# Attention in front of two dense layers on one core: half-height TensorE tiles for units 3 to 11, a new written order, and 40 dummy matmuls

## The chip, the cores and the metric

The kernel runs on one core of one Trainium2 chip, in one launch. The metric is the device time of that core in microseconds (us). A core has five engines that each work through their own queue in order: TensorE (PE, matmuls; its weight loads are listed as PEld), VectorE (DVE), ScalarE (ACT), GpSimd (POOL) and SyncE (SP, which issues most DMAs).

## The reference

```
# 4 batches, 8 heads, 576 positions, head size 64; q and k are drawn 8 times larger
scores = (q @ k.T) / 8
mask:  heads 0-3: 0 <= i-j < 32;  heads 4-7: 0 <= i-j < 128 and (i-j) % 4 == 0
x = softmax(where(mask, scores, -1e9)) @ v          # -> 2304 tokens x 512
h = x @ moe_w_in                                    # 512 -> 2048
x = (h - tanh(h)) @ moe_w_out                       # 2048 -> 512
a, b = x @ moe2_w1, x @ moe2_w2                     # 512 -> 1024 each
out = ((a * b) @ moe2_w3) @ moe2_w_out              # 1024 -> 1024 -> 512
```

q, k and v are float32; the weights come as 64-bit words and are turned into float32 on the chip.

## The kernel before, in words

**Units.** Attention is cut into 12 units: 4 batches times 3 blocks of 192 query positions (3 tiles of 64). Each unit does all 8 heads, as two types: `p` (plain heads 0 to 3) and `d` (dilated heads 4 to 7). A type has two pairs of heads (`e`), a pair has two heads (`h`). A query tile of 64 is handled as two halves of 32 (`half`), and each half looks at a window of 64 keys.

**Steps of a unit**, each a letter in the written order. `q` and `v` load keys with queries, and values (SP). `s` computes scores (lines 480 to 512): one bfloat16 matmul with an identity writes the mask into a PSUM bank, then 24 float32 matmuls for a type add the scores, each in a column tile of 32 (`tile_position=(0, 32*j)`, four of them). The queries lie zero-padded over 128 rows (64 of one head, 64 of the other), so a matmul uses all 128 rows although half of its weights are zeros. A float32 matmul is two instructions in the trace, so a type is 48 and a unit 96. `M` takes the row maximum and subtracts it (DVE), `E` is the exponential (ACT), `N` sums and inverts (DVE), `m` multiplies (POOL), `T` transposes on TensorE (3 per type), `C` copies the transposed weights out of PSUM (lines 568 to 577), twice per type: each copy multiplies by a 0/1 column of `sel_sb`, so that the rows of the other pair are zero. `P` multiplies by the values (lines 579 to 596): 12 float32 matmuls per type with 128 rows, 64 columns and 64 moving elements (24 instructions). `X` and `L` split the result into a rounded part and a rest in the big tile `X` (ACT, DVE).

Units 0 to 2 (`n < PB`) run one type at a time; from unit 3 on `s`, `M`, `E`, `N` and `m` take both types in one step, and the two score banks belong to one tile `both`.

**The first dense layer** is cut into 4 groups of the hidden size. Group 0 has 3 chunks and 8 token tiles, 24 steps: `h` (12 matmuls), `t` tanh (ACT), `g` difference (DVE), `G` rounded part (ACT), `k` rest (POOL), `y` (12 matmuls into the output banks), `Y` and `Z` (bank to SBUF). `h0` needs the attention of batch 0, which is units 0 to 2; `h6` needs that of units 3 to 5, and so on. Group 0 runs interleaved with attention, by hand. Weights for groups 0 and 1 are prepared in the same stretch: `w` load, `a` absolute value (ACT), `b` two and `c` two passes over the bits (DVE, lines 149 to 162), `i` rounded part (ACT), `o` rest (POOL).

**What sets the order.** The string `ORDER` (lines 49 to 69) has 504 words; `first_group` (lines 756 to 817) emits them one after the other, and each engine runs its own in that order. There is no scheduler behind it: a word that waits holds up all later work of its engine. `S<n>` (`spin`, line 750) exists but is not used in this order: it takes an `h` bank and writes `n` bfloat16 matmuls of 512 columns into it that nobody reads. After group 0 loops write the steps: groups 1 to 3 (to about 470 us), eight products of the two last weight matrices (to 521 us), then three passes over token pairs.

**The h banks.** `h_tile` (lines 624 to 627) counts its calls in `nh`. Until `Q0` (`close_attn`) all calls get the one bank of pool `hA`. From then on a call whose count is a multiple of 4 gets `hA`, the others one of three banks of `yB["h"]` in turn. The last eight calls are the eight products (line 935); each is read by ACT (line 945) and DVE (line 946). Line 967 then takes the banks for the last stage, the `hA` bank first; the first matmul of the last stage writes into it.

**PSUM in attention.** `bank_of` (lines 468 to 478) places the scores of units 0 to 2: the first two in the two banks of pool `psS`, the next two in the `y` banks, the last two in `psS` again, which waits until both earlier ones are read.

Of the kernel before, what the change touches and what calls it, by code (L numbers as in the profile page):

```python
# [8 lines left out]
F32 = mybir.dt.float32  # L9
# [26 lines left out]
R = 4  # L36
# [14 lines left out]
N2p T1p v0p s1d v1p m2p s2d w1 a0 E0d C1p T2p b0 P0p C2p N0d c0 M1d X0p M2d E1d v2p a1 m0d L0p b1  # L51
T0d q3p E2d P1p C0d w2 a2 q3d P2p N1d c1 m1d T1d s3 N2d C1d i0 m2d i1 T2d b2 c2 v0d v1d X1p L1p w3
P0d o0 X2p L2p o1 X0d i2 M3 P1d L0d X1d E3 a3 L1d q4p q4d h0 v2d s4 N3 C2d P2d w4 b3 t0 g0 h1 G0 c3
i3 X2d M4 t1 a4 m3p T3p k0 o2 L2d q5p E4 q5d g1 o3 y0 w5 h2 v3p q6p G1 s5 C3p v3d b4 c4 t2 k1 m3d
T3d g2 q6d i4 o4 a5 N4 C3d h3 m4p M5 t3 E5 b5 P3p c5 v4p T4p v4d C4p y1 N5 X3p L3p g3 P3d G2 X3d m4d
T4d i5 k2 C4d L3d s6 M6 q7p q7d o5 P4p v5p X4p L4p h4 t4 m5p y2 Y2 G3 E6 P4d X4d w6 g4 h5 T5p Z2 C5p
m5d s7 N6 G4 L4d v5d P5p k3 y3 t5 g5 a6 X5p G5 T5d C5d w7 k4 a7 b6 k5 v6p m6p L5p y4 h6 M7 q8p t6
T6p c6 g6 q8d y5 q9p C6p i6 h7 G6 v6d E7 b7 t7 c7 g7 P5d N7 k6 w8 G7 Y5 m6d s8 q9d X5d P6p X6p Z5
T6d k7 h8 v7p m7p y6 L5d C6d P6d t8 M8 a8 E8 g8 G8 q10p m7d h9 N8 m8p X6d v7d T7p C7p s9 T7d o6 k8
t9 g9 y7 C7d h10 M9 t10 L6p g10 T8p G9 v8p E9 i7 N9 b8 P7p L6d X7p w9 y8 h11 k9 m8d L7p Y8 q10d s10  # L60
q11p G10 t11 C8p m9p P7d g11 q11d Z8 X7d P8p X8p L7d L8p T8d k10 y9 G11 M10 h12 c8 y10 E10 k11 C8d
t12 v8d m9d v9p a9 v9d y11 w10 T9p C9p g12 h13 G12 P8d b9 Y11 k12 Z11 t13 N10 m10p g13 T9d m10d G13
s11 M11 P9p X8d L8d C9d X9p k13 c9 E11 y12 w11 T10p h14 y13 C10p T10d t14 g14 a10 b10 G14 P9d k14
N11 m11p L9p C10d v10p h15 t15 v10d y14 g15 G15 Y14 h16 v11p T11p t16 k15 Z14 g16 y15 X9d o7 L9d G16
k16 m11d P10p X10p h17 C11p c10 t17 v11d P10d g17 G17 y16 L10p X10d T11d C11d h18 a11 t18 P11p X11p
L10d L11p P11d k17 X11d w12 g18 y17 L11d Y17 b11 Q0 i8 G18 i9 c11 h19 Z17 k18 t19 o8 g19 h20 G19 h21
w13 t20 y18 k19 i10 y19 h22 g20 t21 g21 G20 G21 k20 i11 k21 y20 a12 h23 b12 o9 a13 b13 t22 g22 G22
o10 o11 Z20 k22 Y20 h24 c12 t23 c13 g23 i12 y21 G23 y22 o12 k23 i13 y23 t24 g24 G24 o13 k24 Z23 Y23
"""


# [9 lines left out]
def attn_moe_kernel(  # L81
# [358 lines left out]
    def window(t, half):  # L440

        return 32 * half if t else 0

    def load_v(n, parts=AB):
        if n < NU:
            b, g = units[n]
            for ty in parts:
                v = v_home(n).rearrange("p (h t c) -> p h t c", h=2, t=TU)
                for e in range(2):

                    for t0, t1 in ((0, 1), (1, TU)) if g == 0 else ((0, TU),):
                        src = vt[b, 2 * ty + e, :HW, TU * g + t0:TU * g + t1].rearrange("k t c -> k (t c)")
                        ap = [list(d) for d in src.ap]
                        step = ap[0][0] * window(TU * g + t0, 1)
                        nc.sync.dma_start(
                            out=v[e:128:2, :, t0:t1].rearrange("k h t c -> k h (t c)"),
                            in_=bass.AP(tensor=src.tensor, offset=src.offset, ap=[ap[0], [step, 2], ap[1]]),
                        )
                vs[n, ty] = v

    NB = 2 * TU

# [16 lines left out]

    def at_scores(n, parts=AB):  # L480
        b, g = units[n]
        if n not in ust:
            ms = attn_pools["sm"].tile([128, 2, 2, NB], F32, tag="ms", name="ms")
            if n == 2:
                pm = Yf[:, KC * NT - 6 * KW - 2 * NB * HW:KC * NT - 6 * KW]
                pm = pm.rearrange("p (u i k e) -> p u i k e", u=2, i=TU, e=2)
            else:
                pm = attn_pools["pp"].tile([128, 2, TU, HW, 2], F32, tag="pm", name="pm")
# [3 lines left out]
        ps = ust[n]["ps"]  # L492
        for ty in parts:
            ps[ty] = bank_of(n, ty)[:, :NB * HW].rearrange("p (i k e) -> p i k e", i=TU, e=2)
            m0 = (M_DIL if ty else M_PLAIN)[g]
            nc.tensor.matmul(
                out=ps[ty], lhsT=id16_sb,
                rhs=mask_sb[:, m0:m0 + TU].unsqueeze(3).to_broadcast([128, TU, HW, 2]),
                start=True, stop=False, skip_group_check=True,
            )  # L500
# [10 lines left out]
                            skip_group_check=True, tile_position=(0, HQ * j),  # L511
                        )

    def of_parts(n, parts):

        s = ust[n]
        if len(parts) == 2:
            both = s["both"][:, :, :NB * HW].rearrange("p u (i k e) -> p u i k e", i=TU, e=2)
            return [(both, s["mx"], s["pm"], [128, 2, TU, HW, 2])]
        return [(s["ps"][u], s["mx"][:, u], s["pm"][:, u], [128, TU, HW, 2]) for u in parts]  # L520

    def at_max(n, parts=AB):
        for ps, mx, pm, shape in of_parts(n, parts):
            both = len(shape) == 5
            mx = mx.rearrange("p u (i e) -> p u i e" if both else "p (i e) -> p i e", e=2)
            nc.vector.tensor_reduce(
                out=mx, in_=ps.rearrange("p u i k e -> p u i e k" if both else "p i k e -> p i e k"), axis=AX.X, op=ALU.max
            )
            nc.vector.tensor_tensor(
                out=pm, in0=ps, in1=mx.unsqueeze(len(shape) - 2).to_broadcast(shape), op=ALU.subtract  # L530
            )

    def at_exp(n, parts=AB):
# [2 lines left out]

    def at_norm(n, parts=AB):
        s = ust[n]
        pm, sm = (s["pm"], s["sm"]) if len(parts) == 2 else (s["pm"][:, parts[0]], s["sm"][:, parts[0]])
        both = len(parts) == 2  # L540
        nc.vector.tensor_reduce(  # L541
            out=sm.rearrange("p u (i e) -> p (u i) e" if both else "p (i e) -> p i e", e=2),
            in_=pm.rearrange("p u i k e -> p (u i) e k" if both else "p i k e -> p i e k"), axis=AX.X, op=ALU.add
        )
        nc.vector.tensor_scalar(out=sm, in0=sm, scalar1=1e-9, scalar2=None, op0=ALU.add)
        nc.vector.reciprocal(out=sm, in_=sm)

    def at_mult(n, parts=AB):
        s = ust[n]
        for u in parts:  # L550
            nc.gpsimd.tensor_tensor(
                out=s["pm"][:, u], in0=s["pm"][:, u],
                in1=s["sm"][:, u].rearrange("p (i e) -> p i e", e=2).unsqueeze(2).to_broadcast([128, TU, HW, 2]),
                op=ALU.mult,
            )

    def at_T(n, parts=AB):
        for u in parts:
# [9 lines left out]
    def at_Tcopy(n, parts=AB):  # L568
        for u in parts:
            pt = ust[n]["pt"][u]  # L570
            pb = ust[n]["pt"][u] = attn_pools["pb"][:, npb[0] % NPB]
            npb[0] += 1
            for e in range(2):
                nc.scalar.activation(
                    out=pb[:, :, :, e], in_=pt.rearrange("p i (j q) -> p i j q", j=4), func=ACTF.Copy,
                    scale=sel_sb[:, e:e + 1],
                )

    def at_pv(n, parts=AB):
# [598 lines left out]
```

## Time and profile before

| | us |
|---|---|
| median of 3 runs (lowest, highest) | 800.28 (800.1, 801.37) |
| the profiled execution, and its span from first to last instruction | 802.01, 800.2 |
| PE busy (matmul instructions) | 779.9 |
| PEld busy | 688.0 |
| DVE busy | 548.1 |
| ACT busy | 292.8 |
| POOL busy | 158.3 |

Busy means that at least one instruction of the engine is under way; a wait is idle time. [...] The time outside the span (802.01 less 800.2) is start and end of the launch.

### The profile page before, as it was taken

Reading aid. Unit: us, or ns where it says so; the run is one execution under the profiler, and the core shown is the slowest. Engines: PE = TensorE matmul, PEld = TensorE weight load, DVE = VectorE, ACT = ScalarE, POOL = GpSimd, SP = SyncE. Lnnn points to the kernel's source line nnn. Section 1 sums busy time; section 2 is a strip of 40 time slices with the busy share of each in tenths; the row PEclk is TensorE's granted clock in tenths of the full one; section 3 lists DMA queues with packets and bytes.
Section 4 is the critical chain, followed back from the end, with each engine's and each line's share of the span. In section 5 each row is a group of like instructions: output and inputs, shape, how many; then the busy total and the mean of one; then the engine's idle time right before and its main releaser. Section 6 shows DMA issues by size and latency. Waiting matters only on the chain.

```text
span 800.2 us, 14174 instructions
## 1 busy us (share of the span) xinstructions
PE 779.9 (97%) x5592; PEld 688.0 (86%) x5592; DVE 548.1 (68%) x909; ACT 292.8 (37%) x546; POOL 158.3 (20%) x153
## 2 busy tenths in 40 slices
PE   5699999999999999999999999999999999999998
PEld 4589999888889888898888898799998999899996
DVE  4998675668888779987888889954454544734431
ACT  3566565443444444444444444321122111311111
POOL 3363343500022001210022223211121111211111
PEclk9799999999999999999999999999999999999999
DMA  9988742114455253632554344296203750156302
GB/s 300 302 247 294 236 155 73 53 53 126 150 160 158 105 162 116 186 119 66 156 155 136 105 134 131 93 340 211 93 1 115 238 187 1 41 181 202 118 1 79
DMA packets 62018, 115.58 MB, mean 144 GB/s; under 512 B 6400, under 2 KB 27008, under 8 KB 61952
## 3 DMA queue, kind: packets, MB, share of 16 engines
q1 hardware_dynamic: 61664, 114.32, 44.8%
q8 instruction: 44, 0.72, 0.4%
q10 hardware_dynamic: 288, 0.36, 0.2%
q14 instruction: 22, 0.18, 0.1%
HBM read 95.26 MB, written 19.40 MB: 143 GB/s over the span
## 4 chain that ended last, share of the span: by engine, by line
PE 89%; DVE 8%; ACT 1%; DMA 1%; issue 1%; ACTq 0%; SPq 0%; DVEq 0%
PE h L635 26%; PE y L725 25%; PE pr L979 22%; PE o L1042 6%; PE pr L1042 6%; PE x L592 2%; DVE a L159 2%; PE s L508 2%; DVE a L162 1%; DVE a L153 1%; PE t L561 1%; DVE a L149 1%; DVE Y L872 1%; DVE ms L541 1%; DMA id_sb<-in_ident 0%
## 5 line engine op out<-in xcount | busy, mean ns | idle before, releaser
L725 PE MATMUL y<-gs,LT 128*128 128x512 f32 (+1 forms) x520 | 121.9, 368 | 0.0
L725 PEld LDWEIGHTS y<-gs,LT 128*128 128x128 f32 x520 | 92.1, 188 | 16.3
L635 PE MATMUL h<-X,LT 128*128 128x512 f32 (+1 forms) x471 | 104.9, 370 | 0.0
L635 PEld LDWEIGHTS h<-X,LT 128*128 128x128 f32 x471 | 82.8, 188 | 15.2
L683 DVE TENSOR_TENSOR th<-h,th 128x512 f32<-128x512 f32 (+1 forms) x83 | 51.3, 618 | 58.5 <-ACT th L677 58.3
L979 PE MATMUL pr<-X 128*128 128x384 f32 x435 | 81.8, 334 | 0.0
L979 PE MATMUL pr<-X,LT 128*128 128x384 f32 x405 | 80.7, 336 | 0.0
L635 PE MATMUL h<-X,w 128*128 128x512 f32 (+1 forms) x381 | 78.8, 352 | 0.0
L677 ACT ACTIVATE th<-h 128x512 f32<-128x512 f32 (+1 forms) x83 | 44.8, 540 | 87.4 <-PE h L635 87.4
L979 PEld LDWEIGHTS pr<-X 128*128 128x128 f32 x435 | 76.2, 188 | 0.5
L159 DVE SCALAR_TENSOR_TENSOR a<-st,a 128x512 uint32<-128x512 uint32 x68 | 75.2, 1107 | 0.3
L979 PEld LDWEIGHTS pr<-X,LT 128*128 128x128 f32 x405 | 71.9, 188 | 1.3
L635 PEld LDWEIGHTS h<-X,w 128*128 128x128 f32 x381 | 62.8, 188 | 10.6 <-DVE th L683 0.2
L690 ACT ACTIVATE gs<-th 128x512 fp32r<-128x512 f32 (+1 forms) x83 | 47.9, 577 | 64.5 <-DVE th L683 57.5
L1016 DVE TENSOR_TENSOR u<-pr,u 128x384 f32<-128x384 f32 x72 | 40.1, 557 | 45.1 <-PE pr L979 38.5
L725 PE MATMUL y<-gs,w 128*128 128x256 f32 (+1 forms) x352 | 70.4, 330 | 0.0
L144 ACT ACTIVATE a<-st 128x512 f32<-128x512 f32 x68 | 45.5, 670 | 59.7 <-DMA st<-in_w 21.0
L992 ACT ACTIVATE cs<-u 128x384 fp32r<-128x384 f32 x24 | 12.6, 526 | 149.4 <-DVE u L1016 149.4
L1034 POOL TENSOR_TENSOR Y<-w,v 128x384 f32<-128x384 f32 x24 | 24.5, 1019 | 212.8 <-DVE w L1016 212.8
L725 PEld LDWEIGHTS y<-gs,w 128*128 128x128 f32 x352 | 54.6, 188 | 6.5
L162 DVE SCALAR_TENSOR_TENSOR a<-st,a 128x512 uint32<-128x512 uint32 x68 | 54.8, 806 | 2.3
L170 POOL TENSOR_TENSOR LT<-a,LT 128x512 fp32r<-128x512 f32 x18 | 25.8, 1436 | 152.2 <-ACT LT L167 152.2
(169 smaller groups left out, 1259.5 us busy)
## 6 DMA issues: line engine op xcount, KB each, us to landing
st<-in_w SPq DMA_DIRECT2D x28, 512.0 KB, 3.5
LT<-p SPq DMA_DIRECT2D x56, 256.0 KB, 4.2
X<-p SPq DMA_DIRECT2D x56, 256.0 KB, 4.7
st<-in_w_in SPq DMA_DIRECT2D x16, 512.0 KB, 4.2
st<-in_w_out SPq DMA_DIRECT2D x16, 512.0 KB, 4.1
q<-in_qz SPq DMA_DIRECT2D x18, 384.0 KB, 5.3
p<-LT SPq DMA_DIRECT2D x26, 256.0 KB, 4.5
v<-in_vt SPq DMA_DIRECT2D x32, 192.0 KB, 4.6
```

The costliest lines, as they stand in the source:

```text
L144: nc.scalar.activation(out=a.bitcast(F32), in_=st[:, :, 1].bitcast(F32), func=ACTF.Abs)
L159: nc.vector.scalar_tensor_tensor(out=a, in0=st[:, :, 1], scalar=0xC0000000, in1=a, op0=ALU.bitwise_and, op1=ALU.bitwise_or)
L162: nc.vector.scalar_tensor_tensor(out=a, in0=st[:, :, 0], scalar=29, in1=a, op0=ALU.logical_shift_right, op1=ALU.bitwise_or)
L170: nc.gpsimd.tensor_tensor(out=lo, in0=a.bitcast(F32), in1=hi.bitcast(F32), op=ALU.subtract)
L635: nc.tensor.matmul(out=ps, lhsT=a[sel[0]], rhs=b[sel[1]], start=(start and i == 0), stop=(i == n - 1), **kw)
L677: nc.scalar.activation(out=th[:, :tn], in_=gst[i][:, :tn], func=ACTF.Tanh)
L683: nc.vector.tensor_tensor(out=th[:, :tn], in0=ps[:, :tn], in1=th[:, :tn], op=ALU.subtract)
L690: nc.scalar.activation(out=gs[:, 0, :tn], in_=th[:, :tn], func=ACTF.Copy)
L725: nc.tensor.matmul(out=y[k], lhsT=wt[sel[0]][:, 128 * k:128 * k + 128], rhs=gs[:, sel[1], tn * m:tn * m + tn], start=(cs[m] == 0 and n == ...
L979: nc.tensor.matmul(out=ps[:, :TP], lhsT=s[e][:, 128 * k:128 * k + 128], rhs=(hi, lo)[f][1][k], start=start and n == 0, stop=n == 5, skip_g ...
L1016: nc.vector.tensor_tensor(out=out, in0=ps[:, :TP], in1=x, op=op)
L1042: nc.tensor.matmul(out=tiles[m], lhsT=cs[e][:, 128 * m:128 * m + 128], rhs=WW[j][f], start=begin and n == 0, stop=end and n == 2,)
```

## The change

Four things change together.

1. From unit 3 on a score matmul uses the 64 rows of its own head alone: `tile_position=(64*h, 32*j)`, so there are eight tiles of 64 rows and 32 columns; the two heads (the two row halves) write to two different banks. The number of matmuls stays 48 for a unit. Rows of the score tile are now (pair, query), columns (tile, type, key).
2. `C` becomes one copy per head without `sel_sb` (2 instead of 4 for a unit). `P` takes both types in one step: 48 matmuls with 64 rows, 64 columns and 32 moving elements instead of 24 with 128 rows and 64 moving elements, on four tiles of 64 x 64; the two types (the two row halves) write to two banks. The value loads fill 64 neighbouring rows instead of every second row.
3. `bank_of` gives units 0 to 2 the banks psS0, y0, y1, psS1, y0, y1.
4. `ORDER` is rewritten: the same words but for `P` (one for a unit from unit 3 on) and nine `S` words with 14, 3, 3, 2, 4, 4, 3, 4 and 3 dummy matmuls, all ahead of `h0`. The first weights are loaded and their bits prepared ahead of the masks; scores of units 3 and 4 both stand ahead of `h0` (before: unit 3 alone), `b3 c3` and `N3` too.

```diff
-K0 K1 q0p q1p s0p q2p q0d M0p q1d s1p E0p s2p s0d M1p N0p m0p w0 T0p E1p C0p N1p M2p q2d M0d E2p m1p
...
-P0d o0 X2p L2p o1 X0d i2 M3 P1d L0d X1d E3 a3 L1d q4p q4d h0 v2d s4 N3 C2d P2d w4 b3 t0 g0 h1 G0 c3
...
+w0 q0p q1p w1 q2p q0d a0 b0 K0 K1 c0 S14 s0p s1p s2p q1d q2d a1 w2 M0p v0p E0p M1p i0 b1 c1 s0d M2p
+N0p E1p E2p m0p i1 M0d v1p s1d E0d N1p m1p a2 S3 T0p M1d C0p N2p E1d m2p s2d q3p q3d v2p S3 T1p P0p
+C1p S2 T2p C2p N0d M2d X0p w3 m0d b2 P1p N1d q4p m1d s3 o0 o1 X1p c2 L0p L1p T0d C0d v0d a3 S4 T1d
+P2p E2d X2p S4 P0d q4d v1d M3 E3 S3 s4 v2d b3 c3 i2 L2p C1d N2d N3 X0d m2d w4 P1d L0d X1d q5p m3p S4
+T2d C2d L1d a4 S3 h0 M4 t0 g0 P2d q5d T3p b4 E4 o2 w5 i3 N4 G0 m3d h1 s5 C3p o3 t1 k0 T3d g1 v3p v3d
...
     def bank_of(n, ty):
 
-        if n >= PB:
-            return ust[n]["both"][:, ty]
         m = order0.index((n, ty))
-        if 2 <= m < 4:
-
-            return yA.tile([128, 2, 256], F32, tag=f"y{m - 2}", name=f"s{m}").rearrange("p a c -> p (a c)")
-        if m % 4 == 0:
+        if m % 3:
+            y = yA.tile([128, 2, 256], F32, tag=f"y{m % 3 - 1}", name=f"s{m}")
+            return y.rearrange("p a c -> p (a c)")
+        if m == 0:
             banks0["s"] = attn_pools["psS"].tile([128, 2, 512], F32, tag="s", name="s")
-        return banks0["s"][:, m % 2]
+        return banks0["s"][:, m // 3]
...
+    def scores_by_rows(n, g):
+
+        ps = ust[n]["both"][:, :, :NB * HW].rearrange("p h (i u k) -> p h i u k", i=TU, u=2)
...
+        for i in range(TU):
+            t = TU * g + i
+            for ty in AB:
+                k, q = kq[ty]
+                for h in range(2):
+                    r = slice(64 * h, 64 * h + 64)
+                    for e in range(2):
+                        for half in range(2):
+                            k0 = KS[t] - KS[TU * g] + window(t, half)
+                            j, c = 2 * e + half, QT * h + HQ * half
+                            nc.tensor.matmul(
+                                out=ps[HQ * j:HQ * j + HQ, h, i, 1 - ty], lhsT=q[r, e, i, c:c + HQ],
+                                rhs=k[r, e, k0:k0 + HW], start=False, stop=(i == TU - 1 and ty == 1),
+                                skip_group_check=True, tile_position=(64 * h, HQ * j),
+                            )
...
     def at_Tcopy(n, parts=AB):
...
+            if n >= PB:
+                pb = ust[n]["pt"][u] = pb.rearrange("p i j e q -> p (i j e q)")[:, :TU * 128]
+                nc.scalar.activation(out=pb, in_=pt.rearrange("p i c -> p (i c)"), func=ACTF.Copy)
+                continue
...
     def at_pv(n, parts=AB):
...
+        for i in range(TU):
+            for half in range(2):
+                for e in range(2 if n >= PB else 0):
+                    for ty in AB:
+                        r = slice(HW * (1 - ty), HW * (1 - ty) + HW)
+                        for h in range(2):
+                            c = 128 * i + QT * e + HQ * half
+                            nc.tensor.matmul(
+                                out=x_part(n, ty, i, half, h)[:, e], lhsT=v[e][r, half, i, D * h:D * h + D],
+                                rhs=s["pt"][h][r, c:c + HQ], start=True, stop=True,
+                                tile_position=(r.start, 64 * h),
+                            )
```

## Rows read from the trace of the kernel before

**Rows 1.** The page: busy tenths of PE, DVE and granted clock in 40 slices.
```profile
PE   5699999999999999999999999999999999999998
DVE  4998675668888779987888889954454544734431
PEclk9799999999999999999999999999999999999999
```

**Rows 2.** Busy time by stretch: us, then each engine's busy time (instructions), PEclk, DMA.
```profile
0.00:36.85 36.85, 21.29 (x530) 16.60 (x530) 26.26 (x52) 15.11 (x30) 12.23 (x24) 0.89 0.93 297
36.85:60.00 23.15, 22.74 (x488) 20.29 (x487) 21.56 (x37) 15.27 (x31) 13.18 (x13) 0.95 0.83 260
60.00:157.45 97.45, 97.45 (x1400) 89.76 (x1399) 65.11 (x114) 57.08 (x125) 40.60 (x41) 1.00 0.52 167
...
30.00:40.00 10.00, 7.45 (x97) 6.24 (x92) 8.96 (x14) 5.09 (x11) 3.21 (x3) 0.54 0.97 322
```

**Rows 3.** Timeline of PE, 34 to 44 us: start, us, line, out<-in, count, idle before.
```profile
34.10 2.83 PE L592 MATMUL x<-pb,v 128*64 128x64 f32 x48 [2.55 <-DVE X L619]
36.85 2.83 PE L635 MATMUL h<-X,WG 128*128 128x256 f32 x12
39.53 0.50 PE L496 MATMUL s<-mask_sb,id_sb 128*128 128x384 bf16 x2
39.96 1.55 PE L508 MATMUL s<-k,q 128*32 128x64 f32 x96
41.44 0.92 PE L592 MATMUL x<-pb,v 128*64 128x64 f32 x24
42.28 1.69 PE L635 MATMUL h<-X,WG 128*128 128x256 f32 x12
43.81 0.49 PE L561 MATMUL t<-id_sb,pm 128*128 128x128 f32 x3
```

**Rows 4.** The chain that ended last, end of group 0: start, us, what.
```profile
149.24 8.21 PE y L725 x36
157.45 2.72 PE h L635 x12
```

**Rows 5.** Timeline of DVE, 37 to 40 us.
```profile
37.50 0.56 DVE L619 TENSOR_TENSOR X<-x,X 128x384 fp32r<-128x384 f32 x1 [0.59 <-ACT X L614]
38.23 0.95 DVE L541 TENSOR_REDUCE ms<-pm 128x12 f32<-128x768 f32 x1 [0.17 <-ACT pm L535]
...
39.57 0.36 DVE L149 TENSOR_SCALAR a<-a 128x512 f32<-128x512 f32 x1
```

**Rows 6.** Groups of instructions, 0 to 135 us: count, busy us, mean ns, idle before.
```profile
L162 DVE SCALAR_TENSOR_TENSOR a<-st,a 128x512 uint32<-128x512 uint32 x12 | 13.0, 1086 | 0.4
L159 DVE SCALAR_TENSOR_TENSOR a<-st,a 128x512 uint32<-128x512 uint32 x12 | 10.2, 847 | 0.2
L153 DVE TENSOR_SCALAR a<-a 128x512 uint32<-128x512 uint32 x12 | 7.7, 644 | 0.4
L149 DVE TENSOR_SCALAR a<-a 128x512 f32<-128x512 f32 x12 | 4.9, 406 | 0.4
L144 ACT ACTIVATE a<-st 128x512 f32<-128x512 f32 x12 | 8.0, 667 | 0.8 <-DMA st<-in_w_out 0.8
```

**Rows 7.** DMA issues, 0 to 60 us: count, KB each, median us to landing.
```profile
st<-in_w_in SPq DMA_DIRECT2D x4, 512.0 KB, 5.5
```

**Rows 8.** Weight loads by form, 40 to 130 us: count, busy us, mean ns.
```profile
L592 PEld LDWEIGHTS x<-pb,v 128*64 128x64 f32 x456 | 14.7, 137 | 2.3 <-DVE th L683 0.3 <-DVE a L149 0.2 <-issue 0.2
L508 PEld LDWEIGHTS s<-k,q 128*32 128x32 f32 x768 | 11.2, 110 | 2.6 <-issue 1.9 <-DMA q<-in_qz 0.3 <-DMA v<-in_vt 0.3
...
L635 PEld LDWEIGHTS h<-X,w 128*128 128x128 f32 x72 | 8.8, 188 | 0.3 <-DVE th L683 0.2
```

**Rows 9.** Timeline of all engines, 520 to 523.5 us.
```profile
520.88 1.21 PE L979 MATMUL pr<-X,LT 128*128 128x384 f32 x6
...
521.08 0.60 ACT L945 ACTIVATE w<-h 128x512 fp32r<-128x512 f32 x1 [3.25 <-PE h L635]
...
521.71 0.69 DVE L946 TENSOR_TENSOR LT<-h,w 128x512 fp32r<-128x512 f32 x1 [0.89 <-ACT w L945]
```

More of the change, by code (lines that the diff above doesn't have):

```diff
@@ L55 @@
[L55 to L64, printed above, removed]
@@ L444, in load_v @@
     def load_v(n, parts=AB):
[L445 to L459, printed above, removed]
+        if n >= NU:
+            return
+        b, g = units[n]
+        for part in parts:
+            v = v_home(n).rearrange("p (h t c) -> p h t c", h=2, t=TU)
+            for other in range(2):
+                if n < PB:
+                    rows, ty, e = slice(other, 128, 2), part, other
+                else:
+                    rows, ty, e = slice(HW * other, HW * other + HW), 1 - other, part
+                for t0, t1 in ((0, 1), (1, TU)) if g == 0 else ((0, TU),):
+                    src = vt[b, 2 * ty + e, :HW, TU * g + t0:TU * g + t1].rearrange("k t c -> k (t c)")
+                    ap = [list(d) for d in src.ap]
+                    step = ap[0][0] * window(TU * g + t0, 1)
+                    nc.sync.dma_start(
+                        out=v[rows, :, t0:t1].rearrange("k h t c -> k h (t c)"),
+                        in_=bass.AP(tensor=src.tensor, offset=src.offset, ap=[ap[0], [step, 2], ap[1]]),
+                    )
+            vs[n, part] = v
     NB = 2 * TU
@@ L492, in at_scores @@
         ps = ust[n]["ps"]
+        if n >= PB:
+            scores_by_rows(n, g)
+            return
         for ty in parts:
@@ new lines, in at_max @@
+    def at_max(n, parts=AB):
+        s = ust[n]
+        if n >= PB:
+            ps = s["both"][:, :, :NB * HW].rearrange("p h (b k) -> p h b k", k=HW)
+            pm = s["pm"].rearrange("p h (b k) -> p h b k", k=HW)
+            nc.vector.tensor_reduce(out=s["mx"], in_=ps, axis=AX.X, op=ALU.max)
+            nc.vector.tensor_tensor(
+                out=pm, in0=ps, in1=s["mx"].unsqueeze(3).to_broadcast([128, 2, NB, HW]), op=ALU.subtract
+            )
+            return
+        for u in parts:
+            ps, pm = s["ps"][u], s["pm"][:, u].rearrange("p (i k e) -> p i k e", i=TU, e=2)
+            mx = s["mx"][:, u].rearrange("p (i e) -> p i e", e=2)
+            nc.vector.tensor_reduce(out=mx, in_=ps.rearrange("p i k e -> p i e k"), axis=AX.X, op=ALU.max)
@@ L538, in at_norm @@
         s = ust[n]
[L539 to L546, printed above, removed]
+        for sm, pm in ([(s["sm"], s["pm"])] if n >= PB else [(s["sm"][:, u], s["pm"][:, u]) for u in parts]):
+            if n >= PB:
+                out, src = sm, pm.rearrange("p h (b k) -> p h b k", k=HW)
+            else:
+                out = sm.rearrange("p (i e) -> p i e", e=2)
+                src = pm.rearrange("p (i k e) -> p i e k", i=TU, e=2)
+            nc.vector.tensor_reduce(out=out, in_=src, axis=AX.X, op=ALU.add)
+            nc.vector.tensor_scalar(out=sm, in0=sm, scalar1=1e-9, scalar2=None, op0=ALU.add)
+            nc.vector.reciprocal(out=sm, in_=sm)
     def at_mult(n, parts=AB):
@@ L577, in at_Tcopy, with x_part @@
                 )
+    def x_part(n, ty, i, half, h):
+        x = ust[n]["x"][ty][64 * h:64 * h + 64]
+        if ty:
+            return x[:, :, QT * i + HQ * half:QT * i + HQ * half + HQ]
+        return x.rearrange("p e (r c l) -> p c e l r", r=R, l=HQ // R)[:, 2 * i + half]
     def at_pv(n, parts=AB):
```

82 lines of the change are left out of this document (42 added, 40 removed).

## The prediction, made before the changed kernel was run

> **What bounds the kernel now.** I read the page's slices first [rows 1]: TensorE is at 9 tenths in 37 of 40 slices, so the time is PE's queue, and anything that doesn't shorten or unblock that queue is worth nothing. The exception is the first 40 us: PE is at 5 and 6 tenths there, and the second slice has a granted clock of 0.7. The table by stretch [rows 2] says who holds it up: up to 36.85 us PE is busy 21.29 us, DVE 26.26, and DVE's missing ten lie at the very start; in 36.85 to 60 DVE is busy 21.56 of 23.15 us, PE 22.74; from 60 to 157.45 PE is busy all the time, DVE two thirds of it. So there are three regimes: DVE-bound until the first dense step, both close to full until 60, PE alone from then on. The change touches nothing behind 157.45, where group 0 ends [rows 4], but the counter of the h banks. All of its effect must show as an earlier or later end of group 0, and as one wait near 521 us.
>
> PE's timeline at the border [rows 3]: the values of unit 2 wait 2.55 us for DVE's L619 (step `L`), then run at the lower level (30 to 40 us have a mean clock of 0.54), and `h0` starts at 36.85.
>
> **Part 1: the order ahead of h0.** DVE sets h0, so I count DVE's work ahead of it. Before: 26.26 us up to 36.85, plus what is left of the steps `L` of unit 1 that end at 38.06 [rows 5], some 0.6: 26.9 us. The new order puts `b3 c3` (0.41 + 0.64 + 0.85 + 1.09 = 2.98 us [rows 6]) and `N3` (38.23 to 39.57, 1.34 us [rows 5]) in front as well, and moves nothing of DVE's behind: 31.2 us. In return DVE starts earlier. The first weights are the first DMA in the queue; a load of 512 KB lands within 5.5 us [rows 7], ACT's pass takes 0.67 [rows 6], so `b0` starts at 5 to 7 us, I take 6, where before DVE stood idle for most of the first 12. Idle gaps of 1.2 us, as DVE had them from 14 us on before, put the end of DVE's part at 6 + 31.2 + 1.2 = 38.4 us against 38.06. h0 starts some 1.2 us ahead of that end, now as before (its first matmuls need only the rounded parts): **+0.4 us**, between -0.8 (start at 5, no gap) and +3 (start at 7, gaps of 3: the first queries now come behind 512 KB of weights).
>
> In exchange the scores of unit 4 move ahead of h0 into a pause of PE: 39.53 to 41.44, **-1.9 us** off the dense part [rows 3]. All other PE words on each side of h0 are the same.
>
> **Part 2: the dummies.** `h0` took 39.53 - 36.85 = 2.68 us at the lower level; a later step of the same form takes 43.81 - 42.28 = 1.53 [rows 3]. If the dummies keep the clock at 1.00 until h0: **-1.2 us**, between 0 and -1.2. What the clock gives back ahead of h0 is worth nothing, since DVE sets h0. Their own time hides in pauses: 14 run before any input is there, 26 stand in a stretch in which PE was busy only 21.29 of 36.85 us, part of that at half speed. If one stands in front of real work it costs at most its own word, 4 matmuls.
>
> **Part 3: the tiles.** A block of scores (96 instructions) takes 41.44 - 39.96 = 1.48 us, 15.4 ns each, on four column tiles; a block of values (24) takes 42.28 - 41.44 = 0.84 us, 35 ns each, on two [rows 3]. Times the number of tiles that is 62 and 70 ns per pass and tile: the number of tiles sets the rate, tiles run beside each other. Eight tiles for scores then give 62 / 8 = 7.7 ns, 96 x 7.7 = 0.74 us; I take -0.7 us a unit. Bounds: 0 (the row halves take turns) and -0.74. It counts for units 5 to 11 only, seven, since units 3 and 4 stand ahead of h0: **-4.9 us**, bounds 0 and -5.2.
>
> Values: 96 instructions on four tiles instead of 48 on two (1.68 us a unit). If a pass of half width still costs what it costs now, 62 / 4 = 15.5 ns, 1.49 us; if half, 0.75. What decides is the weight load, which is as wide as before and comes twice as often. Loads of 32, 64 and 128 columns take 110, 137 and 188 ns [rows 8]: (188 - 110) / 96 = 0.81 ns a column, so 64 columns occupy a tile for 52 ns, longer than half a pass. 52 / 4 = 13 ns, 96 x 13 = 1.25; between that and 1.49 I take 1.35: -0.33 us a unit, nine units: **-3.0 us**. Bounds: -0.85 a unit, -7.6 in all (half price), and 96 x 32 = 3.1 us, +1.4 a unit, +12.6 in all (loads of the two row halves take turns).
> [...]
>
> ACT loses two copies a unit, and all steps of M, E, N and m keep their number and size. They lie beside PE; I count nothing. The bank order of units 0 to 2 works ahead of h0 and is in part 1.
>
> **Part 4: what the faster PE runs into.** In 36.85 to 60 us DVE was busy 21.56 of 23.15 us [rows 2]. PE can run ahead there by 1.6 us at most, and its savings in that stretch (scores of unit 4 moved, two blocks of scores, two or three of values, the warm h0) are about 5. The part that is lost is won back in so far as the two new DVE words ahead of h0 (4.3 us) are gone from here. I take **+1.4 us** of new waits, between 0 and +4. Behind 60 us DVE needs 65.11 of 97.45 us, and PE would still need some 90: room enough, but for single waits on the one h bank, which are in those bounds.
>
> **Part 5: the h banks.** Nine `S` words call `h_tile` nine times. So the counter is not left as it was: 9 is 1 modulo 4. In the dense loops four banks in turn are four banks in turn. But the last of the eight products, which had the third bank of `yB["h"]`, now gets the `hA` bank, the one that the last stage writes first. Before, the first matmul there came at 520.88, with no wait [rows 9]. Now it waits for ACT's L945 (521.08, 0.60) and DVE's L946 (521.71 to 522.40): **+1.4 us**, between 0 (another word of the queue covers it: none does, the products are next) and +1.6.
>
> **Sum** from the profiled execution's 802.01 us (span 800.2): +0.4 - 1.9 - 1.2 - 4.9 - 3.0 + 1.4 + 1.4 = **-7.8 us**, so 794.2. That execution lies 1.7 above the median of the runs, 800.28; the runs are what is compared, so 792.5.
>
> **Rivals.**
> A. Values at half price too. For it: 62 and 70 ns a pass are what streams of 64 cost, and nothing in the rows shows a load as the limit. Against: the slope of the loads. Then -7.6 instead of -3.0: -12.4, 788.
> B. The gain is eaten. Either the row halves take turns for the scores, -7.8 + 4.9 = -2.9, 797.4; or h0 comes 2.6 us later still (its upper bound, +3) and new waits cost 2.6 more (+4), -7.8 + 5.2 = -2.6, 797.7; or both, +2.3, 802.6. For it: DVE is full until 60 us and has 4.3 us more to do ahead of h0. Against: it then has less behind it.
> C. Slower, by one mechanism: loads into the two row halves take turns, so values cost 3.1 us a unit and scores gain nothing. Place: every `P` from unit 3 on. It decides as soon as a value instruction costs over 62 / 4 + 5 = about 21 ns. Then +12.6 for values, 0 for scores, no new waits, +1.4 for the bank: +0.4 - 1.9 - 1.2 + 12.6 + 1.4 = +11.3, 811.5. For it: no row shows a tile of 64 rows, and PEld is busy 89.76 of 97.45 us. Against: column tiles do run beside each other.
> [...]
> E. It doesn't do what it says: the dummies miss the pauses in which the clock falls, h0 is as slow as before: +1.2, 793.7. Inside the range.
>
> **Chances.** My forecast, with E: 0.49, its own range 789.5 to 797. A (785 to 789.5): 0.17. B (797 to 802.6): 0.19, of which 0.09 lies within 0.2% of 800.28 (1.6 us, about what a measurement of this kernel can tell from no change), 0.09 below and 0.01 above. C: 0.09, D: 0.01, other stalls of the same sign: 0.05. So faster 0.49 + 0.17 + 0.09 = 0.75, same 0.09, slower 0.16. The range 785 to 803 leaves out C, D, most of the other stalls and a little of A on the far side.
>
> **What would show it.** Scores of units 5 to 11: 96 instructions in about 0.75 us, not 1.48. Values: 96 in about 1.35 us; 0.75 is A, 3 is C. h0 at 37 to 38 us in about 1.5 us, with a granted clock of 1.00 from the first scores on. End of group 0 at 157.45 - 9.2 = about 148 us, and a wait of PE for DVE's L946 of about 1.4 us ahead of the first product of the last stage. The lengths of the stretches behind that stay as they are. Wrong it would be if group 0 ends later than 152, or if PE waits for DVE more than 4 us between h0 and 70 us.

## The result: slower by 1.1%, where faster by 1% was predicted

The changed kernel took 809.45 us (median of 4 runs, 807.75 to 810.4) against 800.39 for the kernel before, measured beside it (800.1 to 801.37): ratio 1.0109, interval 1.0089 to 1.0128. Predicted were 792.5 and a range of 785 to 803. The profiled run has a span of 807.9 us, 7.7 more than before. Three places hold all of it.

First, `h0`. It starts at 41.01 us instead of 36.85 [rows 3]. PE's timeline of the changed kernel ahead of it (start, us, line, out<-in, count, idle before and what ended it):

```profile
29.71 0.49 PE L598 MATMUL t<-id_sb,pm 128*128 128x128 f32 x3 [2.70 <-POOL WG L170]
30.25 0.81 PE L806 MATMUL h<-warm 128*128 128x512 bf16 x3
31.45 0.87 PE L598 MATMUL t<-id_sb,pm 128*128 128x128 f32 x3 [0.39 <-issue]
...
36.57 0.49 PE L527 MATMUL s<-mask_sb,id_sb 128*128 128x384 bf16 x2
36.99 1.17 PE L542 MATMUL s<-k,q 64*32 64x64 f32 x96
38.09 0.92 PE L645 MATMUL x<-pb,v 128*64 128x64 f32 x24
...
41.01 1.69 PE L687 MATMUL h<-X,WG 128*128 128x256 f32 x12
42.62 0.80 PE L645 MATMUL x<-pb,v 128*64 128x64 f32 x19
```

A transpose (`T0d`) waits 2.70 us. The releaser named, GpSimd's L170, is a weight rest that it doesn't read and that had ended at 28.72; GpSimd's multiplication for its own operand had ended at 22.77. Behind it DVE's subtraction for `M3` waits 2.13 us, and all that leads to `h0` comes late. The table by stretch, as in [rows 2], shows that DVE is not what fills the time: it was busy 25.74 us up to 36.85 us, less than before.

```profile
0.00:36.85 36.85, 28.02 (x534) 17.02 (x538) 25.74 (x57) 16.44 (x32) 12.79 (x24) 0.86 0.95 315
36.85:60.00 23.15, 21.94 (x565) 19.12 (x564) 17.80 (x31) 11.41 (x26) 13.58 (x14) 1.00 0.88 245
60.00:157.45 97.45, 92.18 (x1757) 85.44 (x1758) 61.03 (x111) 44.95 (x105) 34.24 (x37) 0.98 0.56 159
```

Second, the dense part. From 60 to 157.45 us PE was busy all the time before; now 5.27 us are missing, and the waits of PE from 41 to 163 us (engine, line, what for, us, times, longest) say that most of them have no releaser in the profile ("issue"):

```profile
PE x L638 <- issue: 2.9, 4, 1.3
PE s L542 <- issue: 1.1, 1, 1.1
PE x L638 <- DMA v<-in_vt: 1.0, 1, 1.0
PE s L542 <- DMA q<-in_qz: 0.7, 1, 0.7
PE h L687 <- DVE X L671: 0.6, 1, 0.6
```

The timeline shows where the first of them stands: in the middle of a block of values, not at its head, where a missing operand would show.

```profile
55.64 1.17 PE L542 MATMUL s<-k,q 64*32 64x64 f32 x96
56.74 1.69 PE L687 MATMUL h<-X,WG 128*128 128x256 f32 x12
58.36 0.55 PE L638 MATMUL x<-pb,v 64*64 64x32 f32 x22
60.19 1.35 PE L638 MATMUL x<-pb,v 64*64 64x32 f32 x74 [1.28 <-issue]
61.47 2.67 PE L777 MATMUL y<-gs,w 128*128 128x256 f32 x12
...
68.12 1.70 PE L777 MATMUL y<-gs,WG 128*128 128x256 f32 x12
```

Group 0 ends at 163.42 us (155.21 + 8.21) instead of 157.45 [rows 4]:

```profile
155.21 8.21 PE y L777 x36
```

Third, the h bank: the first product of the last stage waits 1.41 us for DVE, as in the prediction's part 5.

```profile
527.04 0.60 ACT L997 ACTIVATE w<-h 128x512 fp32r<-128x512 f32 x1 [3.27 <-PE h L687]
527.67 0.69 DVE L998 TENSOR_TENSOR LT<-h,w 128x512 fp32r<-128x512 f32 x1 [0.90 <-ACT w L997]
528.42 0.79 PE L1031 MATMUL pr<-X,LT 128*128 128x384 f32 x3 [1.41 <-DVE LT L998]
```

So 4.16 us for `h0`, 1.81 for the stretch from `h0` to the end of group 0 (122.41 us against 120.60, though it has less work in it), 1.4 for the bank, and 0.3 spread behind.

**What the stops are.** I counted TensorE's instructions from the start of the trace: weight loads, matmuls, and the few in its queue that only wait for a semaphore or drain (126 of 12,249). The stops that are not at the head of a block stand at numbers 960, 2238, 2750, 3774, 4286 and 4797 (a few records are missing): multiples of 256 apart, to within a unit or two. The DMA queues of the page name the carrier, an instruction queue; before,

```profile
q8 instruction: 44, 0.72, 0.4%
```

and after:

```profile
q8 instruction: 48, 0.79, 0.4%
```

A packet is 0.79 MB / 48 = 16.4 KB. The traces hold 11,332 and 12,249 instructions of TensorE; over 256 that is 44.3 and 47.8: one packet for each 256 of them. In the changed kernel the packet in the stretch 57.7 to 58.9 us (view of the DMA queues: packets, MB, share) is the one ahead of the stop that ends at 60.19:

```profile
q8 instruction: 1, 0.02, 5.8%
```

It ran from 57.75 to 58.86, and TensorE went on 1.33 us later. At the other stops it went on 1.33 to 1.62 us behind such a packet. In the kernel before, up to the end of group 0, the packet of each next piece ended at least 1.86 us ahead of it, and nothing stopped there. I call this theory 1: TensorE's program comes in pieces of 256 instructions, a piece is fetched while the one ahead of it runs, and a stretch with many short instructions uses a piece up before the next has come. Counted from the first instruction of one piece to the first of the next, the stretches behind `h0` that ended in a stop took 3.4 to 5.2 us (4.53, 3.84, 5.15, 4.29, 3.44). The length alone does not decide: the kernel before has a piece of 3.42 us, up to 108.19, that ended without a stop, since its packet had begun 0.44 us ahead of the piece's first instruction. A unit from 3 on has 384 such instructions for attention now (192 for scores, 192 for values), 288 before. No piece was fetched far ahead, though no run shows what sets this: taking packets and pieces in their order, no packet began more than 40 instructions (before) or 45 (changed) ahead of the first instruction of the piece before its own; in the changed kernel from 41 to 115 us it began from 0.8 us ahead of it to 3.0 us behind it. The prediction had no term for it.

### The profile page after: what moved, and what is told of

It is laid out like the page before. It is cut to its first block, busy times and chain, and to the rows that moved or that the text cites. A ratio compares the mean times of both kernels' runs of the same rounds, so it can differ in the third digit from the quotient of the medians.

```text
span 807.9 us, 15071 instructions
## 1 busy us (share of the span) xinstructions
PE 786.8 (97%) x6059; PEld 687.8 (85%) x6064; DVE 541.0 (67%) x909; ACT 281.7 (35%) x528; POOL 156.5 (19%) x153
## 4 chain that ended last, share of the span: by engine, by line
PE 89%; DVE 5%; DMA 3%; issue 1%; ACT 1%; SPq 1%; POOL 0%; ACTq 0%; POOLq 0%
PE h L687 26%; PE y L777 24%; PE pr L1031 22%; PE o L1094 6%; PE pr L1094 6%; PE x L638 2%; DMA Y<-in_qz 1%; DVE a L159 1%; PE s L542 1%; PE t L598 1%; DMA q<-in_qz 1%; DVE a L162 1%; DMA Y<-in_masks 1%; DVE Y L924 1%; PE h L806 1%
## 5 line engine op out<-in xcount | busy, mean ns | idle before, releaser
L159 DVE SCALAR_TENSOR_TENSOR a<-st,a 128x512 uint32<-128x512 uint32 x68 | 73.7, 1083 | 0.4
L742 ACT ACTIVATE gs<-th 128x512 fp32r<-128x512 f32 (+1 forms) x83 | 47.8, 576 | 58.9 <-DVE th L735 52.1
L170 POOL TENSOR_TENSOR LT<-a,LT 128x512 fp32r<-128x512 f32 x18 | 24.5, 1363 | 150.2 <-ACT LT L167 150.2
L162 DVE SCALAR_TENSOR_TENSOR a<-st,a 128x512 uint32<-128x512 uint32 x68 | 50.7, 745 | 2.3
```

The lines of the kernel that those rows point to most:

```text
L159: nc.vector.scalar_tensor_tensor(out=a, in0=st[:, :, 1], scalar=0xC0000000, in1=a, op0=ALU.bitwise_and, op1=ALU.bitwise_or)
L162: nc.vector.scalar_tensor_tensor(out=a, in0=st[:, :, 0], scalar=29, in1=a, op0=ALU.logical_shift_right, op1=ALU.bitwise_or)
L170: nc.gpsimd.tensor_tensor(out=lo, in0=a.bitcast(F32), in1=hi.bitcast(F32), op=ALU.subtract)
L742: nc.scalar.activation(out=gs[:, 0, :tn], in_=th[:, :tn], func=ACTF.Copy)
```

## The experiments

The rivals of theory 1, as the expectations number them: theory 2, the 64-row tiles themselves stall PE; theory 3, the new order alone makes `h0` late, by queries that wait behind weights and by GpSimd. Each ratio is against the kernel before, measured beside the run.

**Full-height tiles in the new kernel.** Order, dummies and banks as changed; scores and values as before.

```
-        if n >= PB:
-            scores_by_rows(n, g)
+        (scores, values, masks and copies of the kernel before)
```

> The new order, the dummies and the new bank order, with the full-height tiles of before. Theory 1, instruction supply: TensorE's instructions come in pieces of 256, a piece cannot follow the last one sooner than some 4 us, and the gaps of the changed kernel stand where a piece ends. The first 958 instructions are as many as in the changed kernel, so the gap of some 2.7 us ahead of the transposes of unit 0 (to 29.7 us) stays and h0 starts at about 41 us; after h0 no gap inside a block, since a unit has 288 instructions in place of 384; group 0 ends at 157 to 160 us, 801 to 804 us in all, with the wait of 1.4 us for the h bank. Theory 2, the half-height tiles themselves stall (the row halves get into each other's way): the gap at 29.7 us goes, because the scores ahead of it are full-height here, h0 starts at 38.5, group 0 ends at 155.5, 800 us. Theory 3, the order alone delays h0 (queries behind weights, GpSimd's weight rests ahead of its multiplications): h0 at 41 us by waits for DMA and GpSimd that are no instruction gaps.

804.53 us, just above the 801 to 804 that I expected, ratio 1.0052 (1.0037 to 1.0067). Of the stops behind `h0` one remains at an end of a piece, 0.98 us, and the wait for DVE of 0.61. `h0` is as late (40.92), and the stop ahead of the transpose is still there, at the same instruction number (960), now with no releaser:

```profile
26.20 0.88 PE L508 MATMUL s<-k,q 128*32 128x64 f32 x48 [0.47 <-DMA q<-in_qz]
29.55 0.78 PE L561 MATMUL t<-id_sb,pm 128*128 128x128 f32 x3 [2.47 <-issue]
```

So the 64-row tiles cost some 5 us, and the late `h0` isn't theirs, against theory 2; a stop with no releaser at the same number is not what theory 3 foretold. For the dense part theories 1 and 2 foretold the same here, fewer stops; the narrow matmuls below separate them.

**No dummies.** All nine `S` words out of the order.

```
-... c0 S14 s0p ...   -... a2 S3 T0p ...   (and the other seven)
+... c0 s0p ...       +... a2 T0p ...
```

> The changed kernel without the nine S words (80 TensorE instructions fewer; 44 fewer ahead of the transposes of unit 0). Theory 1: the pieces of 256 end at other places, so the gaps inside blocks move to other blocks (the next ones by 80 instructions), their sum stays 3 to 5 us; the gap ahead of the transposes of unit 0 moves behind them; no wait for the h bank at the last stage (1.4 us less); 803 to 807 us. Theory 2: the gaps stay where they are, 808 us (1.4 less for the bank). Theory 3: h0 at 41 us as before or later, because the clock falls in the pauses.

806.06 us (803.36 to 807.08), ratio 1.0067 (1.0045 to 1.0088). `h0` at 38.46, the bank's wait is gone, and the stops are at other places of the work but again multiples of 256 apart: 1218, 2243, 3266, 4802. The profiled run was the shortest of the four.

**Dummies that don't count.** They take the one bank without `h_tile`.

```
-        ps = h_tile()
+        ps = hA.tile([128, 512], F32, tag="h", name="h")
```

> The changed kernel, with the dummies written into the hA bank without counting a call. All theories: PE's wait of 1.41 us ahead of the first product of the last stage is gone, the rest is the same: 808.0 us, against 809.45. If the bank order matters elsewhere: another difference.

806.42 us, ratio 1.0081 (1.0058 to 1.0104). The first product follows the last matmul of `h` directly:

```profile
523.88 0.40 PE L687 MATMUL h<-LT 128*128 128x512 f32 x1
524.12 1.21 PE L1031 MATMUL pr<-X,LT 128*128 128x384 f32 x6
```

So the counter is the cause of the 1.41 us. The rest of the difference, 1.6 us by the medians and 0.8 by the ratios, isn't settled: the runs of this kernel alone spread over 3.9 us.

**A shift by 112 instructions.** 62 small dummies ahead of everything.

```
         ps = h_tile()
+        if n == 14:
+            n = 8
+            for _ in range(62):
+                nc.tensor.matmul(out=ps[:, :64], lhsT=warm[:, :128], rhs=warm[:, :64], ...)
```

> The changed kernel with 62 small matmuls and 8 of 512 columns in the first dummy word, in place of 14 of 512: 112 TensorE instructions more, all before any input is there. Nothing else moves but the places where a piece of 256 instructions ends. Theory 1: the five gaps inside blocks after 58 us (1.3, 0.5, 0.4, 0.7 and 1.1 us) go or shrink to at most 1.5 us in all, and the gap ahead of the transposes of unit 0 moves; group 0 ends 3 to 6 us earlier, 803 to 806.5 us. Theory 2 and theory 3: the gaps stay at the same instructions, 809 to 810 us.

807.5 us, ratio 1.01 (1.0067 to 1.0132). The stop ahead of the transpose is gone: `T0d` follows the scores directly. The stops came at 1468, 1725, 2493, 4029 and 4285, the same residue modulo 256 in other work (one in the middle of a `y` step). The first, 1.90 us, stands among the dummies just ahead of `h0`, which so starts at 39.59.

```profile
27.40 0.55 PE L598 MATMUL t<-id_sb,pm 128*128 128x128 f32 x3
...
39.16 0.38 PE L810 MATMUL h<-warm 128*128 128x512 bf16 x1 [1.90 <-issue]
39.59 1.70 PE L687 MATMUL h<-X,WG 128*128 128x256 f32 x12
...
95.09 0.84 PE L777 MATMUL y<-gs,w 128*128 128x256 f32 x5 [0.76 <-issue]
```

Behind 41 us the stops at ends of pieces fell only from 4.02 us to 3.63 (all waits from 6.37 to 4.75), not to the 1.5 that I had expected, and the time lies above the expected 803 to 806.5: place right, size wrong.

**As many instructions without 64-row tiles.** The kernel with full-height tiles and dummies, with narrow matmuls ahead of the values, which overwrite their results.

```
+            for c in range(24 if n >= PB else 0):
+                j = c % 4
+                nc.tensor.matmul(out=x[32 * j:32 * j + 32, 0, :8], lhsT=v[:, 0, c // 8, 32 * j:32 * j + 32],
+                                 rhs=s["pt"][ty][:, c // 8, j, 0, :8], ..., tile_position=(0, 32 * j))
```

> The kernel with the new order, the dummies and full-height tiles, with 48 narrow matmuls (32 columns of weights, 8 of stream; their results are overwritten by the values) ahead of the values of each unit from 3 on: as many instructions a unit (384) as with the 64-row tiles, without any 64-row tile. Theory 1 (TensorE's instructions come in pieces of 256 and a dense block of small ones outruns the fetch): the gaps come back, at instruction numbers on one residue modulo 256, 4 to 8 us in all between h0 and the end of group 0 against 1.76 us with full-height tiles alone; with 0.3 to 0.6 us a unit of busy time the runs take 811 to 817 us. Rival (the gaps belong to 64-row tiles): busy time alone is added, gaps stay under 2.5 us, 806 to 810 us.

818.49 us, ratio 1.0236 (1.0207 to 1.0265), longer than either had it. I had miscounted: a float32 matmul is two in the trace, so a unit has 96 narrow ones and 480 instructions, not 384. The span is 13.6 us above that of the full-height kernel: 9 x 96 narrow matmuls at 0.52 / 48 = 10.8 ns, which is 9.4; `h0` 0.9; stops 1.4 (3.14 against 1.76); the remaining 1.9 is unplaced. The stops are where theory 1 has them, at 1982, 3517 and 4797, behind pieces that took 3.26, 3.77 and 4.89 us; the page counts 51 packets for 13,131 instructions (51.3 x 256). All waits together, 3.14 us, are under the 4 to 8 that I expected. So stops at ends of pieces need no 64-row tile, against theory 2; but their sum can't be had from the count alone.

```profile
52.99 0.59 PE L586 MATMUL x<-pb,v 128*32 128x8 f32 x48
53.52 0.45 PE L598 MATMUL x<-pb,v 128*64 128x64 f32 x8
54.90 0.69 PE L598 MATMUL x<-pb,v 128*64 128x64 f32 x16 [0.94 <-issue]
```

**The order alone.** Full-height tiles, no dummies.

> The new order with full-height tiles and no dummies. Theory 1 with the late h0 as a second, separate loss: h0 at 38 to 39 us (as without dummies), gaps at piece ends after h0 under 2 us, the stretch from h0 to the end of group 0 some 118 us against 120.6 before, so group 0 ends at 156 to 157.5 and the runs take 799 to 802 us. Rival (the new order is bad in itself behind h0, by waits for DVE and for loads): group 0 ends at 159 or later, 803 us or more.

798.41 us (798.0 to 799.34, 7 runs), ratio 0.9969 (0.9958 to 0.998): faster than before, and better than the 799 to 802 that I expected. `h0` at 38.57; from there to the end of group 0 it is 115.98 us, 4.6 less than before, with stops of 0.16 us. By the rows three things account for some 4.1 of it: the scores of unit 4 stand ahead of `h0` (1.9), `h0` itself takes 1.85 us instead of 2.68, and the values of a unit are written in one word, 48 in 1.55 us instead of twice 24 in 0.85 (nine units, 1.35). The order was good; both other parts cost more than it gave.

```profile
37.18 0.31 PE L508 MATMUL s<-k,q 128*32 128x64 f32 x5 [0.99 <-issue]
...
38.57 1.92 PE L635 MATMUL h<-X,WG 128*128 128x256 f32 x12
40.42 0.92 PE L592 MATMUL x<-pb,v 128*64 128x64 f32 x24
```

**The second weight load behind the queries.**

```
-w0 q0p q1p w1 q2p q0d a0 ...
+w0 q0p q1p q2p q0d w1 a0 ...
```

> As the run with the order alone, but the second weight load is issued behind the five query loads instead of between them. Theory: the waits for the queries (some 3 us in all before the first masks) set part of the late h0, so h0 comes 0.5 to 1.5 us earlier than with the order alone and the runs are that much shorter. Rival: DVE, which gets its words b1 and c1 later for it, sets h0: h0 no earlier, the same time or up to 1 us longer.

798.5 us (9 runs, 797.85 to 800.45), ratio 0.9976 (0.9966 to 0.9987). In the profile `h0` comes 1.3 us earlier (37.27), as expected; the runs show no gain over the order alone. The profiled run was the shortest of the nine.

**64-row tiles in the old order.** The values of both types at the place of the first, the transposes and copies that they need just ahead.

```
-... m5d s7 N6 G4 L4d v5d P5p k3 y3 t5 g5 a6 X5p G5 T5d C5d w7 ... P5d N7 ...
+... m5d s7 N6 G4 L4d v5d T5d C5d P5 k3 y3 t5 g5 a6 X5p G5 w7 ... N7 ...  (unit 5; the others likewise)
```

> The 64-row tiles from unit 3 on in the old order, without dummies (the values of both kinds of a unit stand where the first of them stood, with the transposes and copies that they need just ahead). Theory 1: h0 at 36.9 as before, scores 1.1 instead of 1.48 us and values 1.5 instead of 1.68 us a block, about -4 us in all, and 3 to 7 us of gaps at piece ends between h0 and the end of group 0: 798 to 804 us. Rival (the gaps need the new order): gaps under 1.5 us, 795 to 797.5 us.

833.32 us, ratio 1.0407 (1.0382 to 1.0433), far from the 798 to 804 that I expected. Useless for the question: the single word makes the values wait for its loads and for DVE.

```profile
PE x L639 <- DMA v<-in_vt: 9.6, 3, 4.5
PE x L639 <- DVE X L672: 7.0, 3, 4.2
```

It shows that these tiles, which need both types of a unit at once, can't simply be put where the first type's values stood; whether another small change of the old order would do is not shown.

**What limits a score block.** The kernel without dummies, with half of the keys left out of the scores of units 3 to 11, so its output is not the attention's.

```
-                                out=ps[..., h, i, 1 - ty], ..., rhs=k[r, e, k0:k0 + HW], ...
+                                out=ps[..., h, i, 1 - ty, :HW // 2], ..., rhs=k[r, e, k0:k0 + HW // 2], ...
```

> The kernel without dummies (new order, 64-row tiles), in which each matmul of the scores of units 3 to 11 streams 32 keys instead of 64; the other half of the keys is left out. It measures what a score block of 96 instructions on eight tiles is limited by. Theory: a pair of weight load and matmul of this size takes some 11 ns of TensorE's own, however many tiles there are (11.5 ns with 64 columns of stream on eight tiles; the narrow matmuls with 8 columns on four tiles took 0.52 us for 48, 10.8 ns): the block stays at 1.05 to 1.1 us. Rival: the tiles of the two row halves partly take turns, so the stream counts: 0.75 to 0.9 us. The whole run as without dummies, 803 to 807 us, by either.

One run, 807.08 us, so the time says little; the block is what counts. An undisturbed block takes 0.95 us from its first matmul to the next word (67.28 to 68.24, both rounded), against 1.10 with 64 columns. Both numbers missed. Half the stream saves 14% of the time: most of it doesn't depend on the stream, but not all.

```profile
67.28 1.02 PE L542 MATMUL s<-k,q 64*32 64x32 f32 x96
68.24 1.70 PE L777 MATMUL y<-gs,WG 128*128 128x256 f32 x12
```

**A few small matmuls at the start, 24 and 48.** On the kernel with the later weight load.

```
-K0 K1 c0 s0p
+K0 K1 c0 S24 s0p     (the other: S48)
-        ps = h_tile()
+        ps = hA.tile([128, 512], F32, tag="h", name="h")
-            nc.tensor.matmul(out=ps, lhsT=warm[:, :128], rhs=warm, start=True, stop=True)
+            nc.tensor.matmul(out=ps[:, :64], lhsT=warm[:, :128], rhs=warm[:, :64], start=True, stop=True)
```

> The new order with full-height tiles and the second weight load behind the queries (h0 at 37.27 us, 798.5), with 24 dummies of 64 columns (48 instructions, under 1 us, before any input is there) that shift all that follows by 48 places. Theory 1 (pieces of 256 instructions): the piece that took 4.9 us up to 30.25 now starts at about 24 us and runs dry at about 27.5, so there is a gap of 0.7 to 2.5 us near 28 to 30 us ahead of the transposes there, and h0 comes 0.5 to 2 us later, at 37.8 to 39.3: 799 to 800.5 us. Rival (places of instructions don't matter): h0 at 37.3, no new gap, 798.5.

> As the run with 24 small dummies, but 48 of them (96 instructions). Theory 1: piece ends fall at about 27, 33.6 and 41 us, none of the pieces up to 60 us lasts under 5 us, the gap of 1.30 us in the scores of unit 4 at 35.88 us goes, and h0 comes about 1 us earlier than without any dummies, at 36 to 36.6 us: 797 to 797.8 us, better than with 24 although more is added. Rival: as with 24, or worse by their own time, 798.5 to 799.

With none, the rows ahead of `h0` are (a stop of 1.30 us within the scores of unit 4):

```profile
35.88 0.31 PE L508 MATMUL s<-k,q 128*32 128x64 f32 x5 [1.30 <-issue]
...
37.27 1.93 PE L635 MATMUL h<-X,WG 128*128 128x256 f32 x12
```

With 24 the stop stands one piece earlier, and `h0` comes 1.16 us later: 799.97 us (10 runs), ratio 0.9993 (0.9984 to 1.0001), as theory 1 had it.

```profile
26.59 1.54 PE L508 MATMUL s<-k,q 128*32 128x64 f32 x95
29.92 0.24 PE L508 MATMUL s<-k,q 128*32 128x64 f32 x1 [1.79 <-issue]
...
38.43 0.74 PE L635 MATMUL h<-X,WG 128*128 128x256 f32 x3
```

With 48, more instructions, the one stop at an end of a piece ahead of `h0` is at 15.47 us, where the next scores wait for queries anyway, and `h0` comes at 36.66, ahead of the kernel without any: 798.37 us (8 runs), ratio 0.9976 (0.9964 to 0.9987).

```profile
32.79 1.55 PE L508 MATMUL s<-k,q 128*32 128x64 f32 x96
35.50 0.92 PE L592 MATMUL x<-pb,v 128*64 128x64 f32 x24 [1.17 <-DVE ms L541]
...
36.66 1.92 PE L635 MATMUL h<-X,WG 128*128 128x256 f32 x12
```

What 24 and 48 do differs by 1.6 us, and the two kernels differ in the number of dummies alone. Not all of it is the stop: with 24 the scores of unit 3 already start 0.57 us later (26.59 against 26.02), behind a granted clock of 0.50 against 0.71 from 20 to 25 us. The other 1.2 us of the 1.77 by which `h0` differs arise from the stop on (1.79 us, and a granted clock of 0.74 behind it, from 30 to 36.66 us), less the 1.17 us that PE waits for DVE with 48. What shows theory 1 is that in all these kernels the stops move to other work with the instructions put in or taken out, and keep their number modulo 256 and their place behind a packet. Against none at all, 48 won 0.6 us in the profile and nothing in the runs, where 797 to 797.8 us had been expected; PE now waits for DVE at the same spot. Three versions (order alone, later load, 48 small ones) beat both kernels at 798.4 to 798.5.

## Why the prediction was wrong, step by step

**The step that failed** is Part 4. It looked for what a faster PE runs into among the other engines ("room enough, but for single waits on the one h bank") and put +1.4 us on it. The runs showed PE stopping for its own program, for which the prediction's sum had no term. Of 6.37 us of stops behind `h0` 4.02 stand at ends of pieces, 1.74 are waits for loads of values and queries and 0.61 the wait for DVE; with full-height tiles 0.98, 0 and 0.61 are left. Each costs 0.2 to 0.3 us more than the idle time shown, since idle starts at the modelled end of the last matmul: the block of values at 58.36 took 3.11 us from first matmul to next word, 1.53 + 1.28 + 0.30. And behind the longest one the work ran slower: the `y` at 61.47 took 2.67 us, the one at 68.12 1.70. The clock fell there: it was granted in full (1.00) from 58.00 to 61.47 us, a stretch in which PE was busy 0.91 of the first 2.19 us, then 0.56 up to 64.42 (0.50 from 62.00 on) and 0.80 up to 66.40.

**Part 3** had the tiles' own gain too large. A score block takes 1.10 us instead of 1.48, -0.38 and not -0.7: 11.5 ns a matmul, while 62 / 8 had given 7.7. "The number of tiles sets the rate" held from two tiles (35 ns) to four (15.4). The narrow matmuls, with an eighth of the stream on four tiles, took 10.8 ns: this suggests, without showing it, that near this size a pair of load and matmul has a price of its own. An undisturbed block of values takes 1.53 us (50.47 to 52.00), close to the 1.49 of a pass of half width that costs as much as a full one; I had taken 1.35. And the comparison was wrong: the order's single word does 48 full-height ones in 1.55, so the tiles gave 0.02 a unit. The change cut the values' stream from 64 to 32 and doubled the number of instructions, and the block kept its time. On four tiles of 32 columns a shorter stream did take less: 10.8 ns with a stream of 8, 15.4 with 64. The weight loads of 64 rows, which no row of before showed, cost what those of 128 rows did (134 ns against 137, 105 against 110 [rows 8]). Rival C, loads that take turns, did not happen: a block of values took 1.53 us and not 3.

```profile
L638 PEld LDWEIGHTS x<-pb,v 64*64 64x64 f32 x768 | 12.7, 134 | 5.6 <-issue 3.7 <-DMA v<-in_vt 1.1
...
L542 PEld LDWEIGHTS s<-k,q 64*32 64x32 f32 x672 | 7.2, 105 | 4.4 <-issue 2.9 <-DMA q<-in_qz 0.9 <-DMA k<-in_kT 0.3
```

Tiles in all: predicted -7.9, measured +4.9 in the end of group 0 (158.54 to 163.42).

**Part 1** missed by 3.8 us: +4.16 instead of +0.4, past the bound of +3. DVE was not what set `h0`. Without dummies it is +1.72, in which a stop of 0.99 us at an end of a piece is contained (37.18 in that trace) and the queries behind the weights count too: with the second load later, +0.42. The -1.9 for the scores of unit 4 was right. Two slips of the working change nothing in this: the values that wait at 34.10 [rows 3] are `P0d` and `P1d`, not those of unit 2, and a start at 5 without gaps gives -1.9 (5 + 31.2 against 38.06), not -0.8, as the lower bound.

**Part 2** had the gain nearly right and the price wrong. `h0` took 1.61 us instead of 2.68, -1.07. But the order alone takes 1.85, so 0.24 of it are the dummies'. "Their own time hides in pauses" held for their time (from the transpose `T1d` to `h0` it is 9.1 us with them and 9.4 without), not for their places in the program: with them `h0` comes 2.35 us later (38.57 to 40.92), and `T0d`, which stood right at the end of a piece, 2.21 (27.34 to 29.55). With the dummies and a shift by 112 instructions `T0d` is back at 27.40: this shows that the stop there comes from its place. Of the 5.7 us that the dummies cost in all, 2.35 are this, 1.6 lie between `h0` and the end of group 0 (117.62 us against 115.98, nearly all of it waits), and 1.4 are the bank.

**Part 5** was right: 1.41 us against 1.4, and gone without the count.

In steps, the order gave -2.9 us in the spans (800.2 to 797.3), the dummies took 5.7 (803.0) and the tiles 4.9 (807.9). In the runs the same steps are 0.9969, 1.0052 and 1.0109. What happened is what the chances had as "other stalls of the same sign", 0.05. Rival B, a gain that is eaten, ended at 802.6 and named causes that did not happen; C (811.5) came near in time for a reason that the blocks exclude. What stays open: why the next piece comes 3.3 us behind the start of the one ahead at one place and 5 or 7 at another, so that neither the shift by 112 nor the narrow matmuls had the sum of stops that I had expected. The stretches ahead of 60 us have DMA shares around 0.9, but no run varied that alone.

## What to carry over

Count TensorE's instructions per microsecond, not only its busy time: where 256 of them (loads and matmuls) pass in some 3 to 5 us, as ahead of the stops in the dense part here (3.44 to 5.15), the next piece may not be there, and a finer tiling that saves time per block can lose it at the ends of pieces. Read such a stop by its place: within a block, "issue" or a releaser long done, a multiple of 256 instructions from the last one, 1.3 to 1.6 us behind the end of a 16 KB packet of the instruction queue. Time parts of a change apart before they are joined: here the order alone was worth 0.3%, and the two parts beside it took back more than four times that.

## What was unexpected in the hardware

- TensorE stopped at ends of pieces of 256 instructions, six times in the changed kernel up to the end of group 0 (numbers 960 to 4797). The next piece ran 1.3 to 1.6 us behind the end of its packet (0.9 to 1.6 us for 16 KB, amid other transfers). Behind the first instruction of the piece ahead this was 3.4 to 5.2 us at the five stops behind `h0`, 5.8 at the one ahead of it, and 7.1 with the order alone (the stop up to 37.18).
- Where the program's pieces ended decided microseconds: 24 small matmuls in dead time cost some 1.4 us by the ratios (0.9993 against 0.9976), 48 cost nothing.
- Matmuls on eight 64x32 tiles came every 11.5 ns with 64 columns and every 9.9 ns (0.95 / 96) with 32.
- The kernels with 64-row tiles spread over 2.7 to 5.4 us from run to run and the one with narrow matmuls over 4.8; the kernel before spread over 1.3 to 2.5, the others over 1.3 to 2.9. Why is open.
